# Two products of one transform unit in a single VectorE instruction, in a newly ordered plan

## The chip, the cores and the metric

The kernel runs on one core of one Trainium2 chip. The metric is the device time of one launch in microseconds. The kernel before the change took 190.81 us, the median of three runs (190.63 to 191.04).

## The reference

Two branches read the same normalised input and are multiplied at the end.

```python
xn = layernorm(A_q)                                  # [1, 2048, 640]
# branch A: a short causal convolution of k, times v, then a long convolution
k_shift = sum over t of k_pad[:, t:t+S, :] * shift_k[:, 3-t]
kv = k_shift * v
y  = irfft2(rfft2(kv padded to 2S) * rfft2(ssm_k padded to 2S))[:S]
s  = xn * (y + kv * ssm_D)
# branch B: a dense layer with gelu, a second one, then silu
h  = gelu(xn @ w1 + b1)                              # 640 -> 1728
g  = silu(h @ w2 + b2)                               # 1728 -> 640
out = A_q + s * g
```

All tensors are bfloat16; S is 2048 and D is 640.

## The kernel before, in words

The long convolution is done as a transform written as matrix products. A first stage (steps `kf` for the filter, `uf` for the signal) multiplies by sine and cosine matrices; its results go to DRAM scratch (`ks`, `us`) and come back transposed (`fl`, `ml`). A second stage works in 40 units of 128 x 512. For the filter, `ff` is a unit's transform on TensorE and `fe` its copy from PSUM to SBUF, which makes `K`. For the signal, `mu` is the transform; its result is multiplied with two things: with `K` (step `mp`, `product_a`) and with `ks`, which is `K` with neighbouring partitions exchanged (step `mq`, `product_b`). The exchange is done by two DMAs on the SyncE queue (step `mk`, `swap_load`). The two products then go through the inverse transform, `ma` on the first and `mb` on the second, which add up in one PSUM bank; `me` copies that out, `ms` stores it to scratch on GpSimd's queue, `yl` loads it back on SyncE's queue, and `y` is the last transform. `yt` multiplies it with the input, `yo` adds, `ys` and `gs` store.

Unit `i` covers 512 columns of a pair of half-slots. When `i % 5 == 2` it straddles two slots, and its operand has two pieces of 256. When `i % 3 == 2` ScalarE first copies `mu`'s PSUM bank to SBUF (`mv`, `u_copy`), and both products read that bfloat16 copy; for the other 27 units both products read PSUM in float32.

The second-stage matrices are block-diagonal, four blocks of 32 x 32. So each of `ff`, `mu`, `ma` and `mb` is four small matmuls (`blocks`, line 451), called a quad here. The string `TURNS` gives each unit a digit that says which of the four column groups each row group writes; quads with different digits use different tiles of the array. The dense branch fills the rest of TensorE: `h` is one column block of the first layer (line 504, or 500 for the last block of a chunk), `he` its gelu on ScalarE, `g` a row block of the second layer (line 537), `ge` its silu on ScalarE, `gm` the product on VectorE or GpSimd. The input comes in four chunks: `ls`, `lv`, `lr`, `lb`, `ln` normalise one, `tt` and `te` transpose it. `cv` are the 32 large VectorE steps of the short convolution. `kt` and `kc` transpose the filter.

The order of all work is written out by hand in the string `PLAN`: about 1,100 steps, each a kind, a number and, after a dot, the engine or form (`.a` ScalarE, `.d` VectorE, `.p` GpSimd for copies and products; `.f` and `.q` for quads, which act alike unless the digit is 0 and the form `f`). Each engine and each queue issues its instructions in the order in which the plan names them; semaphores hold them until their inputs are there. Eight PSUM banks (`ones`) and 48 SBUF slots (`Slots`) are handed out while the plan is read, first freed first granted, so the order of the plan also decides who waits for whose buffer.

```python
def copied(i):
    return i % 3 == 2
def one(key):
    return banks[:, ones.take(key, 2 if key[0] == "mu" and not copied(key[1]) else 1), :]
```

Of the kernel before, what the change touches and what calls it, by code (L numbers as in the profile page):

```python
# [38 lines left out]
ke13.a kc12.d gm1.d kf37 kc3.a kf5 kt13 X3 kt15 kc7.d kf3 kf30 ke37.a kf4 kc2.d kf23 ke12.a K1 kc13.d kf31 ke3.a ke4.a
d kt11 kt6 gm0.d kc15.d kt8 ke31.a ke30.d kc11.a kt9 kc6.d kc8.d kc9.a ke5.d kt14 kc14.d kt5 kf34 V1 ke23.a kf35 kf18  # L40
K2 V6 kf26 kc5.d kt0 ke34.a kf14 ke26.a kc0.d ke14.a kf33 kf38 kf45 ke45.a kf43 ke43.a g3 V4 kf15 ke35.a kf36 cv6 ks1
ke33.a kf2 V2 kf22 ke18.a ge3 kf1 ke38.a ke2.a ks11 kf0 ke1.a cv16 kf21 ke0.a g5 ke15.d ke22.a V0 kf44 ke36.a ir ke21.a
cv17 kf46 ge5 gm3.d kf10 ke10.a kf32 kf16 kf17 ke44.a ks12 cv18 ke16.a ks0 kf19 ke32.a cv7 ke19.a ke46.a g7 kf9 kf7
# [10 lines left out]
ue47.a ue42.d ue41.a fl4 us15 ue39.a us14 ue40.a ls11 ue21.d uf37 ls8 ue37.a g13 ff8.f fl7 gm6.d ff0.f lv2 ge13 fe0.a
ff6.q ff19.f ff24.q ff5.q fe5.d us12 ff9.q ls13 g9 fe9.a us7 lr2 fe24.a fl5 ff14.q fe19.a ff11.f ge9 lb2 ff18.q ln11.d
fl14 fl12 fe14.d gm8.d ff28.f fe18.a fe28.d fe8.a fe6.a us13 ln10.d mk3 g15 fe11.a ff13.q ln9.a fl6 fe13.a ff29.q ml3
ff35.f ml2 ff10.q ff34.q ff26.q fe26.a mk2 gm13.p fe35.a ln8.d g10 tt12 ge15 fe34.d fe10.d tt11 tt14 tt13 fe29.a ls15
ff2.f ff36.q ge10 te14.a ff32.q ff23.f ml4 te12.d te11.d te13.d ff30.f ls14 ff33.f fe2.a gm15.p ff12.q fe23.d fe32.a
fe30.a fe12.a mk5 ff3.f g11 ff15.q ff16.q ls12 ff17.q fe3.a fe36.d fe33.a ge11 tt10 fe15.d fe16.a ff1.q fe17.a lv3 lr3
mu8.q ff4.q te10.d mu9.f gm11.p fe4.a ff20.q mu7.f mu5.f mq9 fe1.d mv8 mq7 h30 ml5 mv5 h31 h34 mk4 mp9 mu6.q fl15 lb3  # L60
ff25.f ml0 mp5 mp8 mu11.q he30 fe20.d mk1 mu12.q he31 ma9.f ff22.q mp7 mq5 mb9.f mq6 he34 h38 mu10.f fe25.a mv11 me9.a
mp6 ff21.q mk0 fe22.a ma7.f ff37.q fe21.a gm10.p ln12.d mp12 mp10 mb7.f he38 mq10 mu14.q ln13.d mv14 mp11 me7.a fe37.a
h35 h33 ma5.q mu1.q mq12 ln14.d mb5.f ml6 mu0.f he35 ma10.f mu13.q mq1 he33 ff38.q fe38.a me5.a ma6.f mb6.f ml1 mp14
mp1 ml8 mp0 mb10.q h41 me10.a ml12 he41 me6.a h28 mq0 h36 mu3.f he28 ff39.q ml13 mu20.q mu2.q he36 mu4.f mp13 h32 mq13
mk6 ff31.f mk8 mv20 mq3 mk13 mp3 ma3.f mq14 mv2 ma0.f mu15.f fe39.a ml9 mu32.f mb3.f mb0.f ml10 mk9 he32 me0.a mq4
fe31.a mk12 me3.a h29 mp2 h37 mk7 mq15 h39 mv32 ma2.q mq11 he29 mu33.f ma14.q q6 ma12.f mp4 he37 he39 mq2 mb14.q mp15
mp32 mu23.f mq8 mb2.f mb12.f ml15 h40 mp20 mv23 ml14 me2.a mq33 mp33 mu30.q ln15.d me12.a mp23 me14.a mu21.q ma1.q
ma8.q ma11.q mq21 mb1.q mb8.q mb11.q tt16 te16.d mk10 he40 me1.a g17 tt15 mp21 mq20 mu31.q me8.a mp30 mu22.q mq30
# [21 lines left out]
def kernel(  # L90
# [85 lines left out]
    REACH = 24  # L176

    class Slots:
# [40 lines left out]
    def flat(key, uses=1):  # L219
        return rows_of[:, slots.take(key, uses), :]  # L220
# [35 lines left out]
    def full(ap, i):  # L256
        return ap if i % PER != PER // 2 else ap.rearrange("p (a b) -> p a b", a=2)
# [456 lines left out]
    def product(i, x):  # L714
        name = ("K", "ks")[x]
        u = p_part(i, 1) if copied(i) else full(one(("mu", i)), i)
        nc.vector.tensor_tensor(out=p_part(i, x), in0=u, in1=span(name, i), op=ALU.mult)  # L717
# [239 lines left out]
```

## Time and profile before

| what | value |
|---|---|
| median of three runs | 190.81 us |
| profiled execution | 190.82 us |
| its span, first to last instruction | 189.0 us |
| granted TensorE clock | 0.996 |
| TensorE busy | 182.8 us, 97% |
| VectorE busy | 166.6 us, 88% |
| ScalarE busy | 158.5 us, 84% |
| GpSimd busy | 62.3 us, 33% |

The profiled execution took 190.82 us, of which 189.0 us are the span; so 1.8 us lie outside it. Busy time of VectorE and ScalarE counts from an instruction's start to the end of its last write; the next instruction can start before that. So the distance from one start to the next, called the pitch below, is shorter than the duration, and it is the pitch that says how much work an engine gets through.

### The profile page before, as it was taken

How to read it: one execution, taken by the hardware profiler on the slowest of the kernel's cores; microseconds unless marked ns; L12 is line 12 of the kernel's file. 1: busy time of each engine (PE TensorE's matmuls, PEld its weight loads, DVE VectorE, ACT ScalarE, POOL GpSimd, SP SyncE). 2: the span in 40 equal slices, each digit the busy share in tenths (PEclk: the TensorE clock that was granted, in tenths of full speed). 3: DMA queues.
4: the chain of work that ended last, by engine and by line, in shares of the span. 5: the costliest groups of instructions: out<-in, count | busy, mean ns of one | idle time of the engine just before them, and what ended most of it. 6: DMA issues, size and time to landing. Idle time of an engine off the chain costs nothing.

```text
span 189.0 us, 4812 instructions
## 1 busy us (share of the span) xinstructions
PE 182.8 (97%) x1808; PEld 110.2 (58%) x1808; DVE 166.6 (88%) x317; ACT 158.5 (84%) x309; POOL 62.3 (33%) x98
## 2 busy tenths in 40 slices
PE   6899999999999999999999999999999999999992
PEld 2486468977764455665653344465645544677671
DVE  7979899999999999999999999999999600489993
ACT  3757999899999999999999999999898989952021
POOL 8545200029845104157216000030596620010320
PEclk9999999999999999999999999999999999999998
DMA  5999999959899899989789999699799869992545
GB/s 188 376 370 314 347 398 410 358 166 395 329 361 364 287 321 381 297 337 350 236 263 278 341 316 328 229 360 332 234 342 326 317 201 300 394 399 94 212 160 188
DMA packets 26399, 57.67 MB, mean 305 GB/s; under 512 B 3016, under 2 KB 14857, under 8 KB 26376
## 3 DMA queue, kind: packets, MB, share of 16 engines
q1 hardware_dynamic: 21872, 39.65, 61.1%
q0 software_dynamic: 4320, 17.70, 25.4%
q8 instruction: 14, 0.23, 0.5%
q14 instruction: 9, 0.07, 0.1%
q10 hardware_dynamic: 184, 0.01, 0.1%
HBM read 33.76 MB, written 18.35 MB: 276 GB/s over the span
## 4 chain that ended last, share of the span: by engine, by line
PE 85%; DVE 5%; DMA 4%; ACT 3%; issue 1%; SPq 0%; DVEq 0%
PE banks L537 31%; PE banks L504 24%; PE banks L588 9%; PE banks L451 7%; DMA w_sb<-in_B_w_dram 4%; PE banks L832 4%; PE banks L577 3%; PE banks L759 2%; PE banks L760 2%; DVE area L146 2%; PE banks L488 1%; ACT area L145 1%; DVE area L717 1%; PE banks L500 1%; DVE st L458 1%
## 5 line engine op out<-in xcount | busy, mean ns | idle before, releaser
L145 ACT CAST area<-banks 128x512 bf16<-128x512 f32 (+2 forms) x153 | 74.5, 592 | 2.8 <-PE banks L451 1.8
L537 PE MATMUL banks<-w_sb,hT 128*128 128x320 bf16 (+1 forms) x462 | 65.7, 295 | 0.0
L537 PEld LDWEIGHTS <-hT 128*128 128x128 bf16 x462 | 43.7, 98 | 18.1 <-issue 1.9
L504 PE MATMUL banks<-xnT,w_sb 128*128 128x512 bf16 x230 | 53.3, 379 | 0.1
L504 PEld LDWEIGHTS <-w_sb 128*128 128x128 bf16 x230 | 21.7, 98 | 26.7 <-issue 3.5
L516 ACT ACTIVATE hT<-banks,b_f 128x512 bf16<-128x512 f32 x52 | 32.7, 707 | 2.8 <-PE banks L832 1.7
L717 DVE TENSOR_TENSOR area<-banks,area 128x512 bf16<-128x512 f32 x54 | 34.6, 686 | 0.1
L545 ACT ACTIVATE sl<-banks 128x320 bf16<-128x320 f32 (+1 forms) x33 | 14.6, 451 | 14.8 <-PE banks L537 12.9
L553 POOL TENSOR_TENSOR xn<-xn,sl 128x320 bf16<-128x320 bf16 x13 | 10.6, 827 | 48.9 <-ACT sl L545 26.0
L641 DVE TENSOR_TENSOR area<-area 128x2560 bf16<-128x2560 bf16 x16 | 23.5, 1485 | 0.6 <-DMA area<-in_A_k_dram 0.5
L768 DVE TENSOR_TENSOR area<-banks,xn 128x426 bf16<-128x426 f32 (+1 forms) x18 | 10.0, 596 | 14.0 <-PE banks L760 14.0
L451 PE MATMUL banks<-area,mats 32*32 32x512 bf16 x640 | 18.8, 380 | 0.6 <-DVE area L146 0.5
L637 DVE TENSOR_TENSOR area<-area 128x2560 bf16<-128x2560 bf16 x12 | 17.9, 1492 | 0.2
L603 POOL DMA_DIRECT2D scrK<-area x16 | 8.9, 560 | 24.3 <-DVE area L146 18.4
L588 PE MATMUL banks<-area,WB 128*128 128x426 bf16 (+1 forms) x64 | 15.5, 299 | 0.0
L614 POOL DMA_DIRECT2D scrU<-area x16 | 8.7, 547 | 20.6 <-ACT area L145 20.6
L588 PE MATMUL banks<-area,WA 128*128 128x428 bf16 (+1 forms) x64 | 15.4, 298 | 0.0
L146 DVE CAST area<-banks 128x512 bf16<-128x512 f32 (+2 forms) x23 | 14.2, 638 | 0.3 <-ACT area L145 0.2
L451 PEld LDWEIGHTS <-mats 32*32 32x32 bf16 x640 | 6.7, 88 | 10.7 <-issue 8.9
L744 POOL DMA_DIRECT2D scrC<-area x16 | 11.7, 734 | 3.0 <-ACT WB L674 1.4
L717 DVE TENSOR_TENSOR area<-area 128x512 bf16<-128x512 bf16 x26 | 10.5, 420 | 0.0
L458 DVE BATCH_NORM_STATS2 st<-xn 128x6 f32<-128x320 bf16 x24 | 10.4, 476 | 0.0
(109 smaller groups left out, 218.6 us busy)
## 6 DMA issues: line engine op xcount, KB each, us to landing
scrK<-area POOLq DMA_DIRECT2D x16, 320.0 KB, 4.1
scrU<-area POOLq DMA_DIRECT2D x16, 320.0 KB, 3.6
area<-scrK SPq DMA_DIRECT2D x16, 320.0 KB, 6.2
area<-area SPq DMA_DIRECT2D x32, 160.0 KB, 4.2
area<-scrU SPq DMA_DIRECT2D x16, 320.0 KB, 5.6
scrC<-area POOLq DMA_DIRECT2D x16, 320.0 KB, 4.5
area<-scrC SPq DMA_DIRECT2D x16, 320.0 KB, 7.0
area<-in_A_ssm_k_dram SPq DMA_DIRECT2D x5, 512.0 KB, 9.0
```

Source lines behind the costliest of these rows:

```text
L145: return nc.scalar.copy(out=out_ap, in_=in_ap)
L146: return nc.vector.tensor_copy(out=out_ap, in_=in_ap)
L451: nc.tensor.matmul(out=out[b, :], lhsT=mats[a, m, a], rhs=rhs[a, :], start=start, stop=stop)
L458: nc.vector.bn_stats(out=st[:, j, h, :], in_=xn_tiles[c][:, j, h * HALF:(h + 1) * HALF])
L504: nc.tensor.matmul(out=ps, lhsT=w1_sb[:, t, ft * P:(ft + 1) * P], rhs=xnT[:, t, :], start=(t == 0), stop=(t == DT - 1))
L516: nc.scalar.activation(out=hT[:, ft, :], in_=one(("h", i)), func=ACT.Gelu_apprx_tanh, bias=b1_f[:, ft:ft + 1], scale=1.0)
L537: nc.tensor.matmul(out=ps[:, 0:ws.stop - ws.start], lhsT=hT[0:M, ft, q * P:(q + 1) * P], rhs=w2_sb[0:M, ft, hs.start + ws.start:hs.start + ...
L545: nc.scalar.activation(out=sl[:, ws], in_=one(key)[:, 0:ws.stop - ws.start], func=ACT.Silu)
L588: nc.tensor.matmul(out=ps[:, dst], lhsT=(WA, WB)[r][:, n2, :], rhs=rows[:, n2 % 2, src], start=True, stop=True)
L637: nc.vector.tensor_tensor(out=uc, in0=uc, in1=tmp, op=ALU.add)
L641: nc.vector.tensor_tensor(out=tmp if s else uc, in0=kh[:, r0:r0 + KR, :].rearrange("p (a b) d -> p a b d", a=2), in1=w_exp[:, j:j + 1, Non ...
L717: nc.vector.tensor_tensor(out=p_part(i, x), in0=u, in1=span(name, i), op=ALU.mult)
```

## The change

For the 32 units with `i % 5 != 2` (`joined`), the steps `mp` and `mq` become one step `mm` (`product_ab`): one VectorE instruction of 128 x 2 x 512, whose first input is the transformed signal repeated twice, and whose second input is a two-piece view of `K` and `ks`. The view needs the two slots within 2^15 elements of each other, so `Slots.beside` picks slots for `ks` near those of `K`; where it finds none, two instructions are used as before. Which of the two lies lower in memory decides the order of the halves (`swapped`). The eight straddling units keep `mp` and `mq`. The plan is a different order of all steps, with other engines for some copies, and `TURNS` is new.

```diff
-TURNS = "303222211332100321313102031211323202233020231231"
+TURNS = "123121012012312302321300020110231032133023221311"
 PLAN = ...   # another order; 1099 steps become 1067
...
+    NEAR = 25
...
+            if key[0] == "ks":
+                got = self.beside(key[1])
+                keys = [(key[0], key[1] & ~1), (key[0], key[1] | 1)]
+            elif key[0] in SPANNED:
...
+        def beside(self, g2):
+            ke, ko = self.at["K", g2 & ~1], self.at["K", g2 | 1]
+            for j in range(1, len(self.free)):
+                for i in range(j):
+                    lo, hi = sorted((self.free[i], self.free[j]))
+                    if hi - lo <= REACH and abs(lo - ke) <= NEAR and abs(hi - ko) <= NEAR:
+                        return [lo, hi]
+            first = self.free[0]
+            return [first, next(s for s in self.free[1:] if abs(s - first) <= REACH)]
...
+    def joined(i):
+        return i % PER != PER // 2
...
+    def product_ab(i):
+        k, ks = span("K", i), span("ks", i)
+        swap = int(ks.offset < k.offset)
+        lo, hi = (ks, k) if swap else (k, ks)
+        if hi.offset - lo.offset >= 1 << 15:
+            product_a(i)
+            return product_b(i)
+        both = bass.AP(lo.tensor, lo.offset, [list(lo.ap[0]), [hi.offset - lo.offset, 2], [1, HB]])
+        u = p_part(i, 1) if copied(i) else one(("mu", i))
+        out = flat(("p", i))[:, 0:2 * HB].rearrange("p (x c) -> p x c", x=2)
+        nc.vector.tensor_tensor(out=out, in0=u[:, None, :].to_broadcast([P, 2, HB]), in1=both, op=ALU.mult)
+        swapped[i] = swap
+        drop_span("K", i)
+        drop_span("ks", i)
```

Of the steps that have a choice of engine, the new plan puts these counts on each:

| step | before | after |
|---|---|---|
| `fe` on ScalarE / VectorE | 29 / 11 | 32 / 8 |
| `me` on ScalarE / VectorE | 39 / 1 | 35 / 5 |
| `ke` on ScalarE / VectorE | 45 / 3 | 44 / 4 |
| `ue` on ScalarE / VectorE | 40 / 8 | 39 / 9 |
| `kc` on ScalarE / VectorE | 4 / 12 | 5 / 11 |
| `ln` on ScalarE / VectorE | 1 / 11 | 0 / 12 |
| `gm` on VectorE / GpSimd | 19 / 13 | 17 / 15 |

More of the change, by code (lines that the diff above doesn't have):

```diff
@@ L39 @@
[L39 to L43, printed above, removed]
@@ L54 @@
[L54 to L58, printed above, removed]
@@ L59 @@
[L59 to L68, printed above, removed]
@@ new lines @@
+kc11.d kt1 kf22 kt15 K1 te5.d kc1.d ke22.a V6 kf21 ke21.d kt2 kc2.d d kt4 kf23 kc8.a kc15.a kf35 ke35.d ke23.a kf33 kt5
+kc4.d kt3 kc3.d ke33.a kf45 kt6 kf34 kc6.d ke45.a kt12 kc12.d kf46 ke34.a kf10 ke46.a kf26 kf8 ke8.a kt9 kc5.d kt10 ks7
+gm0.d kf42 ke26.d kf5 kc9.a X2 kc10.d ke5.a kt0 ks11 kf44 ke44.a kc0.a kf6 cv8 kf9 ke42.a kf7 g7 kf30 cv6 kf47 ke6.a
+ke7.a kf17 kf3 kf4 ks2 ke9.a cv17 ke30.a g1 ge7 kf12 kf13 ke17.a kf31 ke4.a ke3.a ks1 ke47.a X3 ks14 ke10.a kf25 kf32
+kf15 ge1 ke13.a ke31.a V5 kf24 ke24.a g6 kf16 kf19 ke15.a gm7.d V3 kf36 ke32.a cv7 uf5 ke25.a kf38 ke12.a kf20 ke16.a
@@ new lines @@
+ke36.a ue5.a kf14 ke20.a cv16 cv18 cv19 ke14.a kf1 ke19.a K3 ke1.a g2 ke38.a gm5.d kf18 kf29 uf2 kf40 ks15 kf37 ks8
+ke18.a cv9 kf11 g4 ke37.a V7 kf0 ks5 ks4 cv20 ke11.a ue2.a ge2 kf28 gm1.d cv21 cv22 kf27 kf2 ge6 ke29.a V2 ke40.a ke0.a
+ks6 ke27.a ks3 ke2.d uf3 ks12 kf39 h18 kf41 ue3.a ke39.a uf1 cv10 ks10 ke41.a ge4 V4 uf0 cv23 ks0 uf4 ke28.a ue1.a h23
+uf11 ue4.a uf10 ue10.a ue0.d h15 h26 he18 uf7 ue7.a he26 uf9 h24 ks13 he23 ks9 uf33 uf35 ue11.a h22 fl0 fl12 uf30 cv11
+h20 ue35.a he22 he15 ue33.a fl7 uf32 he24 gm6.d uf34 he20 fl3 h19 h21 ue34.a ue32.a cv12 ue30.a he19 uf24 fl1 fl4
@@ new lines @@
+ue24.a he21 fl2 h25 uf27 uf28 ue27.a uf6 ue6.a ue9.a uf31 cv24 us1 cv13 gm2.d he25 ue28.a h14 cv14 he14 cv15 uf19 h16
+uf25 ue19.a fl9 cv25 us0 he16 uf14 h17 us11 uf13 ue14.a uf26 he17 fl8 cv26 cv27 uf8 h27 ue8.a us2 ff7.f ue25.d ue26.d
+fl13 ue31.d ue13.a ff11.f uf29 uf21 uf12 fe7.a ue12.a cv28 he27 g14 uf20 ue21.d cv29 fl15 ge14 uf16 ue20.d uf18 cv30 g9
+ue29.a uf17 us3 ue16.a uf23 us10 uf15 fe11.a us4 uf22 g13 ue18.a cv31 ge9 uf36 ls12 ue15.a ue17.a us8 gm14.p ue22.a
+uf45 ue23.a uf43 ge13 ue45.a ue36.d uf37 us9 uf47 us5 us6 ue43.d uf42 uf38 gm13.p ue37.a ue42.a uf40 us7 ue40.a uf41
@@ new lines @@
+uf46 ue38.a uf44 ue46.a ls8 uf39 g15 ls9 fl10 fl6 ue39.d ue47.a ue44.a ff8.q ff2.q ff5.f ls10 ue41.a gm4.d us15 ge15
+us14 ff9.q fe9.a ff0.f ff34.q fe34.a fe2.a ff22.q ls11 g11 gm15.p us13 fe22.a ff24.q ff10.f fe5.d ge11 ff30.f fl5 us12
+fe8.a ls14 mk3 ff31.q g8 ff18.q fe10.a lv2 fe0.a ls13 ff13.q fe24.a lr2 fe31.a fl11 fl14 ff6.q fe18.a ff25.f g10 fe6.a
+ff4.q ml3 ge8 ff3.f gm11.p ff33.q ff12.f ls15 fe25.d ff1.f lv3 fe30.a gm9.d lb2 fe13.a ln11.d ml2 mk2 ff20.f ge10 fe4.a
+ln8.d g12 ml8 fe1.a fe3.a ln10.d lr3 fe20.d fe33.d lb3 ln9.d tt14 tt12 ln15.d gm8.p ml4 ml5 fe12.a mk4 ln13.d te12.d
@@ new lines @@
+ff26.q ge12 ff14.q te14.a fe14.d ff15.f ml0 fe15.a ff28.q tt13 tt10 te10.d fe26.a mk0 tt11 te11.d ff23.q ff36.f ml1
+fe28.a ff29.q te13.d fe36.a fe23.d ff16.q ff32.f fe16.d fe32.a fe29.a h31 ff37.f ff27.f mk12 fe37.d gm10.p mu9.q mu6.q
+he31 mu7.f mp7 mu8.q mk5 mq7 h28 h39 mm9 fe27.a h29 ma7.f mu10.f mv8 he39 he28 ma9.q ff17.f fe17.a mu14.q mb9.q mb7.f
+mm8 mv14 h30 mm6 h40 mm10 mk1 mu0.f ln12.d me9.a he29 ml13 he30 me7.d ma6.q ma10.f mm0 he40 mu11.f mv11 mb6.q ln14.d
+mb10.f ff21.q ml12 mu1.f h38 me6.a me10.a mu12.q ma8.q mm1 fe21.a mk8 mu5.q ma0.f mb8.q h33 mu4.q mv5 he38 mu3.f mu20.f
@@ new lines @@
+ir me8.a mm11 ml9 he33 mq12 mb0.f me0.a ff19.f h36 mp12 fe19.a mv20 mu2.f mu13.f ff35.f fe35.a h37 mk13 ff38.q ff39.q
+mm4 mv2 mu30.q mm3 ma4.q mu32.f he36 mm14 he37 mm13 mb4.q fe38.a fe39.a mk6 h32 mp2 h35 mk9 me4.a he32 mv32 h34 mm5 mq2
+ma12.f mu33.q he35 mm30 ma5.q mu24.q he34 ml11 ma14.f mm33 mb12.q ml6 me12.a ma13.q mb13.q ma3.q me13.a mk10 ml10 mb3.q
+mb5.f me3.a mb14.f me5.a h41 mm24 ma11.q ml7 mu31.q ma2.q mb2.q me14.a mb11.f mu22.q tt15 q2 mm31 tt18 me11.a gm12.p
+mq22 ms2 te15.d he41 g17 te18.a me2.d ma1.q ma31.q mu15.f ma33.q mk11 mp22 mb33.q mm20 mm15 mu23.q ge17 mv23 mb1.f
@@ new lines @@
+me30.a mp37 ge18 ma16.q mv38 mu28.f ma17.f mb23.q q1 mm29 me23.a ma18.q mm28 mb17.f mb27.f mb16.q mb18.f h50 ma37.f
+ma29.q me27.a ma28.q me18.a ms9 me16.d mb28.f mm38 mb29.q mb37.q me17.a ms6 me28.a ma19.f mu39.q mb19.f me19.a q3
+mu36.f mm35 q7 ms7 g22 ge22 ms12 h48 gm20.p ms10 mm36 me29.a ma36.f ma35.q mm39 ma39.q ma38.f ms11 mb36.f me37.a ip1
+ia1 mb35.f ip3 mb39.q me35.d me36.a mb38.f h55 me39.a ia3 is1 ib1 ic1 ms14 me38.d is3 ib3 g23 h53 ms15 h43 ge23 h45 yl7
+yl6 yl13 ic3 he53 h51 h47 he47 h54 h46 he45 he54 ip2 he46 yl14 he51 he43 h44 he50 h49 yl5 h42 gm23.p he44 he42 he49 yl4
@@ new lines @@
+yl0 y9 h52 y11 he48 he55 y20 y10 ia2 he52 g26 y6 ip0 y7 is2 ia0 is0 y8 yt20 yt9 yl2 yt6 ib0 yt11 ic0 g27 ge26 yt7 y21
+ib2 yl3 yl12 yt8 y19 yt10 yo2.d yo3.d yt19 yt21 gm26.d gm18.p yl1 g28 ic2 ge28 y0 y2 ys3 y1 yt2 yt0 ge27 gm22.p yl9 y4
+yt1 y3 yt3 y5 g30 yo0.d yt5 y18 yl8 y13 ge30 yt4 yo1.d ys1 y14 yl11 y17 gm27.d yt17 yl15 gm28.d y23 y12 yl10 y15 q6
+yt13 yt12 y22 yt23 yt14 g29 yt22 ga31 gm30.d ga26 ys2 y16 ge29 yt15 ga27 ys0 q4 ga30 gs27 yo4.d g24 yt18 ga28 yt16
+yo5.d gs30 ge24 g25 ge25 ys4 gm29.d g31 ga29 gm25.d gm24.d ga25 gs29 ga24 gs25 ys5 ge31 gm31.d gs31
@@ L266, in one @@
     def one(key):
-        return banks[:, ones.take(key, 2 if key[0] == "mu" and not copied(key[1]) else 1), :]
+        return banks[:, ones.take(key, 2 if key[0] == "mu" and not copied(key[1]) and not joined(key[1]) else 1), :]
     def one_bf(key):
@@ L705, in u_f2 @@
         drop_span("uin", i)
+    swapped = {}
     def p_part(i, x):
+        x ^= swapped.get(i, 0)
         return full(flat(("p", i))[:, x * HB:x * HB + HB], i)
@@ L715, in product @@
         name = ("K", "ks")[x]
+        last = x == 1 or not joined(i)
         u = p_part(i, 1) if copied(i) else full(one(("mu", i)), i)
@@ L718, in product @@
         drop_span(name, i)
+        if last and not copied(i):
+            ones.drop(("mu", i))
+    def product_ab(i):
[12 more added lines that the diff above has]
+        drop_span("ks", i)
         if not copied(i):
```

41 lines of the change are left out of this document (9 added, 32 removed).

## The prediction

> **What bounds the kernel now.** I read the page first: the busy shares, the slices, the chain that ended last.
>
> ```profile
> span 189.0 us, 4812 instructions
> PE 182.8 (97%) x1808; PEld 110.2 (58%) x1808; DVE 166.6 (88%) x317; ACT 158.5 (84%) x309; POOL 62.3 (33%) x98
> ...
> PE   6899999999999999999999999999999999999992
> ...
> DVE  7979899999999999999999999999999600489993
> ACT  3757999899999999999999999999898989952021
> ...
> PE 85%; DVE 5%; DMA 4%; ACT 3%; issue 1%; SPq 0%; DVEq 0%
> ```
>
> All three engines are nearly full, VectorE (DVE) until slice 31 (about 149 us), and TensorE (PE) carries most of the chain. So the question is how much of PE's time is work and how much is waiting for the other two. The chain in order of time answers it, since it shows PE's pace for each kind of step:
>
> ```profile
> 16.62 1.08 PE banks L504 x5
> 17.70 0.67 PE banks L500 x10
> ...
> 24.95 0.67 PE banks L488 x12
> ...
> 31.79 1.56 PE banks L577 x25
> ...
> 80.63 1.90 PE banks L537 x14
> 82.53 2.36 PE banks L588 x17
> ...
> 86.80 0.58 PE banks L451 x27
> ...
> 89.44 0.36 PE banks L451 x16
> ...
> 92.47 1.29 DVE area L146 x2
> ...
> 101.47 1.28 DVE area L717 x2
> ...
> 111.25 1.08 ACT area L145 x2
> ...
> 122.81 2.02 PE banks L537 x14
> ...
> 161.42 0.09 PE banks L759
> ...
> 185.44 0.31 ACT sl L545
> ```
>
> The plan's PE work runs from 16.62 to 185.44, 168.8 us. Its work at these paces: 46 `h` of 1.08, 4 short ones of 0.67, 32 `g` of 1.90, 96 units `kf` and `uf` of 0.18 (the 17 matmuls in 2.36 us, four matmuls to three units), 24 `y` of 0.36, 80 transposes of 0.062 and 60 of 0.056: 147.8 us. Then the quads. Four quads with four different digits start together and the run ends after 0.36 us; seven quads, of which digits come twice or thrice, take 0.58. So I count a run of neighbouring quads as 0.32 us after its last start and 0.21 for each time it waits for a digit's tiles to come free, read off `TURNS` in the plan's order. Before has 22 runs, 16.3 us. Sum 164.1: PE would end at 180.75 if it never waited, and it ends at 185.44. **So 4.7 us are waiting**, and no change of VectorE alone can give back more. Where it lies: up to 91 us the chain is on PE; from 92.5 to 114.5 it runs for long stretches over DVE and ACT; step `g17` starts at 122.81, where PE's own work would have brought it at 119.2, 3.6 late. So most of the waiting lies between 92 and 123, when chunk 3 is normalised while the first products run.
>
> **What VectorE has to do.** Its pitch from the timeline, and the groups of the page:
>
> ```profile
> 13.51 1.22 DVE L344 TENSOR_SCALAR area<-area 128x2048 int32<-128x2048 int32 x1
> ...
> 111.47 4.28 DVE L717 TENSOR_TENSOR area<-banks,area 128x512 bf16<-128x512 f32 x7
> ...
> 119.39 1.09 DVE L717 TENSOR_TENSOR area<-area 128x512 bf16<-128x512 bf16 x3
> ...
> 145.41 0.42 DVE L717 TENSOR_TENSOR area<-area 128x512 bf16<-128x512 bf16 x1
> ```
> ```profile
> L717 DVE TENSOR_TENSOR area<-banks,area 128x512 bf16<-128x512 f32 x54 | 34.6, 686 | 0.1
> L641 DVE TENSOR_TENSOR area<-area 128x2560 bf16<-128x2560 bf16 x16 | 23.5, 1485 | 0.6 <-DMA area<-in_A_k_dram 0.5
> L768 DVE TENSOR_TENSOR area<-banks,xn 128x426 bf16<-128x426 f32 (+1 forms) x18 | 10.0, 596 | 14.0 <-PE banks L760 14.0
> ...
> L717 DVE TENSOR_TENSOR area<-area 128x512 bf16<-128x512 bf16 x26 | 10.5, 420 | 0.0
> ```
>
> One product from PSUM lasts 686 ns, but seven take 4.28 us: a pitch of 0.60. From SBUF: 420 ns, three in 1.09, a pitch of 0.33. Adding the pitches of all VectorE steps in the plan's order up to the last product gives 127.8 us (32 `cv` of 1.41 and 80 products of 41.0 together make two thirds). It passed from 13.51 to 145.7, 132.2 us. So VectorE came 4.4 us later than its work asks, and it was never idle long. Its work alone would bring the last product at 141.2; PE's own work needs it at 141.4. Slack of 0.2 us on paper, 4.4 us of lateness in fact: this is where PE's waiting comes from.
>
> **The change, part by part.**
>
> The joined products. From 426 to 512 elements PSUM products grow by 90 ns, 1.05 ns an element; so 1024 elements last 686 + 536 = 1.22 us, pitch 1.13, against 1.20 for two: 0.065 saved on each of 22 units, 1.4 us. From SBUF, 512 to 2560 elements cost 1065 ns more, 0.52 ns each; two products make 0.60 instead of 0.67, 10 units, 0.7 us. Sum 2.1 us, not the 32 x 0.15 that the durations suggest, since the end of one instruction already lies under the start of the next. The bounds: 0 (if the two-piece view costs as much as it saves) and 32 x 0.15 = 4.8.
>
> For this price the Trainium skill, "VectorE: DVE Perf Modes", section "The TRN2 errata", has 58 cycles fixed for an SBUF source and 120 for PSUM. By it the estimate would be 22 x 125 + 10 x 60 ns = 3.4 us, 1.3 more than by the pitch, and the sum below 188.9 instead of 189.6. For SBUF the pitch agrees (65 ns); for PSUM it shows half, and I keep the pitch.
>
> Other steps moved onto and off VectorE before its last product: `me` +3 (1.8 us by a pitch of 0.60), `fe` -3 (-1.8), `ke` and `ue` +1 each (+1.0), `ln` +1 (+0.35), `kc` -1 (-0.4), `gm` -1 (-0.2), one `ip` behind the last product (-0.6). Sum +0.1. So VectorE has 125.9 us before its last product, 1.95 less, and could bring it at 139.4.
>
> The new order for PE. 24 runs of quads instead of 22, with other digits: 16.8 us by the same count, +0.46. This is on PE's path whatever else happens. PE has 125.8 us of work ahead of the last product's matmuls, 1.0 more, so it needs them at 142.4. The slack grows from 0.2 to 3.0 us; for the products from 100 on it is 2.6 to 3.0 wherever it is smallest, against 0.2 to 1.2 before. Only where chunk 3's transposes feed `h31` it shrinks, from 3.1 to 2.1.
>
> ScalarE. Its sum to the end is 1.5 us shorter, but at the start of `g17`, where chunk 3's first layer must be done, its own work stands 2.1 us ahead of PE's need, 2.2 before: no relief where the waiting is. Its pitches:
>
> ```profile
> 143.54 2.06 ACT L145 CAST area<-banks 128x512 bf16<-128x512 f32 x4
> ...
> 156.09 6.06 ACT L516 ACTIVATE hT<-banks,b_f 128x512 bf16<-128x512 f32 x10
> ```
>
> (0.48 and 0.59 us.) GpSimd gets two `gm` more, 1.7 us on an engine a third busy.
>
> Waits that are added. A joined product waits for `ks` as well as `K`, and `ma` waits for 1.22 us instead of the first 0.69; whatever VectorE has queued behind a late `ks` waits too.
>
> ```profile
> area<-area SPq DMA_DIRECT2D x32, 160.0 KB, 4.2
> area<-scrC SPq DMA_DIRECT2D x16, 320.0 KB, 7.0
> ...
> 148.74 2.17 POOL L744 DMA_DIRECT2D scrC<-area  x3 [1.42 <-ACT WB L674]
> ...
> 153.78 8.98 SPq L751 DMA_DIRECT2D area<-scrC  x13
> ```
>
> The exchange lands in 4.2 us. Between the last `fe` of a pair and its first use of `ks` lie 5.6 us of work at least in the new plan (`mk2`, a straddling unit), 8.9 for a joined one; 7.6 at least before. Covered; price 0, and up to 2 us for one that slips. I followed the slot rule through the plan: all 32 units find slots in reach, mostly the first two on the list, so it makes no buffer wait that first-freed would not.
>
> The round trip through scratch C. After the last quad PE has 15.3 us to fill until `y7` at 161.42 (last quad at 146.1). The new plan leaves 13.9. The trip: last stores at 150.2, loads from 153.8, landing 7.0 by the median, so 14.7 with everything; but ScalarE brought that last copy late, at 148.9, and the new plan gives it to VectorE, then idle, about 1.4 us sooner. 13.3 against 13.9: covered, barely. Head and tail (16.6 us ahead of the plan; 3.6 from PE's end to the span's) keep their work.
>
> **The sum.** Waiting now 4.7. By VectorE's slack, if it comes as late as before, 4.4 less 2.6 or 2.1 leaves 1.8 to 2.3; by ScalarE, whose slack is unchanged, about 3.6 at `g17` and 4.0 in all. The chain of 92 to 114 has both, so I take the middle, 3.0: a gain of 1.7. Less 0.46 for the quads: 1.2. PE ends at 184.2, the span is 187.8, and with 1.8 outside it 189.6, 0.6% under 190.82 (the profiled execution stands within 0.01 of the median). The ends of this case: 1.2 us of waiting, 187.8; 4.0 and a little back, 190.4.
>
> **The rivals.**
>
> ScalarE sets the waiting, VectorE's time goes idle. Then 4.0 to 4.7 of waiting plus 0.46: 190.5 to 191.2, no difference. For it: ACT at 9 in every slice from 4 to 30, and its part in the chain at 111. Against: DVE has twice as many pieces there.
>
> Slower: the order's own waits. The trip through C is the place: if the last stores go out as late as before after the last quad, `y` comes 0.8 to 1.4 us late, PE has nothing left to fill with, and with no gain elsewhere the time is 191.3 to 192.6. It decides once stores and loads together take over 13.9 us. For it: a load of C takes 7.0 us, an exchange 4.2. Against: the earlier last copy.
>
> Slower: the ten units from SBUF lose their fast rate, because their first input repeats. At 1.05 ns an element a joined one has a pitch of 1.13, 5.3 us more on VectorE; the slack goes from 3.0 to -2.3, waiting to 6.7 or more, the time to 193.3. It decides when a joined SBUF product lasts over about 1.0 us. Against: L641 repeats its weight row four times and still does 0.52 ns an element. The Trainium skill, same page, section "Mode 2×_1P", asks for 16-bit data and a step of 1, and a repeated half isn't one; the row of L641 speaks for the inner step alone counting.
>
> **How the numbers follow.** Chances: the forecast 0.56; ScalarE rival 0.18; own waits 0.19; lost rate 0.07. 0.2% is 0.4 us, about what can be told here. Faster holds the forecast case and little else, 0.56; same 0.18; slower 0.26. The forecast's own range is 187.8 to 190.4; for 8 in 10 it must reach over the second case and half of the third: 187.7 to 192.0.
>
> **What would show it.** Products of 128x1024 with 1.22 us from PSUM and 0.69 from SBUF; the chain between 92 and 114 more on PE than now; `g17` less late; the last product near 143 instead of 145; quads with 24 ends; `y` following the last `h` without a gap. I'm wrong if VectorE idles in that stretch while PE still waits for ScalarE, if PE waits for a load of C near 160, or if SBUF products last 1.2 us.

## The result, and the profile after

| kernel | median of the runs | profiled execution | its span |
|---|---|---|---|
| before | 190.62 us (190.16 to 191.26) | 190.82 us | 189.0 us |
| after | 192.34 us (191.56 to 193.51) | 192.19 us | 190.4 us |

The change makes the kernel slower: after against before is 1.0087, 95% interval 1.0066 to 1.0109, 1.7 us. The forecast was 189.6. Further on, "after" also gets 192.37 and 192.04 in two more executions. Some executions below were disturbed (`b_joined` and `a_gm` have one of 473 and 373 us, which was the profiled one); these two profiles are not read, and the ratios leave disturbed runs out.

The page of after, the same lines as those shown of before: span, busy shares, slices of PE, VectorE and ScalarE, and the shares of the chain that ended last.

```profile
span 190.4 us, 4799 instructions
PE 182.4 (96%) x1808; PEld 110.7 (58%) x1808; DVE 167.3 (88%) x286; ACT 157.9 (83%) x306; POOL 62.8 (33%) x100
...
PE   7999999999998999999999999999999999999990
...
DVE  7989899999699999999999999899999900499992
ACT  3767998999997999999999999999896978961020
...
PE 53%; DVE 23%; DMA 7%; ACT 7%; issue 5%; SPq 2%; POOL 1%; DVEq 0%; POOLq 0%
```

PE carries 53% of the chain instead of 85%. The larger part of VectorE's 23% lies at the start, up to 33 us, and at the end, where the chain stays on VectorE from 165.60 until the last stores. In between, new are slice 10 of VectorE (a 6, at about 50 us) and slice 12 of PE (an 8, at about 57 us), where before has nines. The chain in order of time says what stands there and in the stages that the prediction read:

```profile
44.49 6.72 DMA scrK<-area
51.33 1.49 DVE area L656
52.82 1.40 DVE area L652
...
57.31 0.61 DVE area L144
57.95 0.52 PE banks L603 x3
...
95.78 0.19 SPq L715
96.03 1.20 SPq L715
97.34 0.52 SPq L709
97.91 5.31 DMA area<-scrU
103.22 1.27 DVE area L736 x2
104.49 1.14 DVE area L751
...
149.90 10.79 PE banks L519 x50
160.70 0.18 PE banks L795
```

The store of scratch K holds VectorE's step `cv9` until 51.33, and six steps later PE. Between 95 and 105 the chain runs through SyncE's queue and a load of scratch U into the products. The last `h` run ends at 160.69 and `y` starts at 160.70: the trip through scratch C is covered.

The products are what was forecast. In the groups by shape of VectorE (busy, mean ns | idle):

```profile
L751 DVE TENSOR_TENSOR area<-banks,area 128x1024 bf16<-128x1024 f32 x22 | 26.1, 1216 | 0.6 <-ACT hT L531 0.6
...
L751 DVE TENSOR_TENSOR area<-area 128x1024 bf16<-128x1024 bf16 x10 | 7.2, 733 | 0.0
```

All 32 joined units are there, 1.22 us from PSUM; the 733 is a mean of nine of 0.68 and one of 1.20, which comes up below. From start to start a joined product takes 1.134 us from PSUM (two single ones 2 x 0.598) and 0.600 from SBUF (2 x 0.333): 0.062 and 0.066 saved, against 0.065 forecast, 2.0 us in all. So VectorE has the time that was promised. Where it went shows in VectorE's waits up to the last product, after and then before:

```profile
DVE area L656 <- ACT area L143: 1.5, 1, 1.5
DVE nb L486 <- POOL rs L482: 0.9, 1, 0.9
DVE area L751 <- ACT hT L531: 0.6, 1, 0.6
DVE area L144 <- ACT area L143: 0.2, 1, 0.2
```
```profile
DVE xnT L146 <- PE banks L823: 0.8, 1, 0.8
DVE area L641 <- DMA area<-in_A_k_dram: 0.5, 1, 0.5
DVE area L146 <- ACT area L145: 0.5, 2, 0.2
DVE b_f L900 <- ACT xnT L145: 0.3, 1, 0.3
```

and in its timeline, beside GpSimd's, at three places of after:

```profile
79.94 1.48 DVE L652 TENSOR_TENSOR area<-area 128x2560 bf16<-128x2560 bf16 x1
81.46 1.96 DVE L645 TENSOR_TENSOR area<-area 128x2560 bf16<-128x2560 bf16 x1
80.17 1.90 POOL L568 TENSOR_TENSOR xn<-xn,sl 128x320 bf16<-128x320 bf16 x1 [1.05 <-ACT sl L560]
...
88.89 0.90 DVE L568 TENSOR_TENSOR xn<-xn,sl 128x320 bf16<-128x320 bf16 x1
88.82 0.79 POOL L568 TENSOR_TENSOR xn<-xn,sl 128x320 bf16<-128x320 bf16 x1 [0.30 <-ACT sl L560]
...
139.54 0.68 DVE L736 TENSOR_TENSOR area<-banks,area 128x512 bf16<-128x512 f32 x1
140.14 1.20 DVE L751 TENSOR_TENSOR area<-area 128x1024 bf16<-128x1024 bf16 x1
139.98 0.81 POOL L568 TENSOR_TENSOR xn<-xn,sl 128x320 bf16<-128x320 bf16 x1
```

A `gm` on VectorE (L568) lasts 0.32 us elsewhere, here 0.90; a joined product from SBUF 0.68, here 1.20; a `cv` step 1.49, here 1.96. Each time a product of GpSimd is running when VectorE's instruction starts. The `cv` at 79.94 was there first: it keeps its 1.48, and GpSimd's product takes 1.90 instead of 0.80. A joined product from PSUM that starts in the middle of one of GpSimd's keeps its 1.22:

```profile
132.51 1.22 DVE L751 TENSOR_TENSOR area<-banks,area 128x1024 bf16<-128x1024 f32 x1
132.37 0.87 POOL L568 TENSOR_TENSOR xn<-xn,sl 128x320 bf16<-128x320 bf16 x1 [5.34 <-DMA area<-area]
```

The Trainium skill, "SBUF — State Buffer", section "Who interferes with whom", says that a VectorE instruction with two SBUF inputs and a GpSimd instruction that reads SBUF exclude each other, and that one with a single SBUF input does not; the trace agrees, with these 0.47, 0.58 and 0.52 us.

VectorE's account from 13.0 us to the end of its last product, from the trace (end taken one pitch after the last start; before 145.41, after 145.34):

| | before | after |
|---|---|---|
| idle | 2.3 | 4.4 |
| held up by a product of GpSimd | 0.3 | 1.6 |
| work | 130.1 | 127.5 |
| last product done at | 145.7 | 146.5 |

2.6 us of work less (1.95 forecast), 2.1 more of waiting, 1.3 more of standing still: 0.8 later in all. PE's last matmul ends at 185.76, before 185.41: 0.35 later. The other 1.0 us of the 1.35 in the span lies behind it. The last stores, issued on GpSimd's queue (L813, before L777) and on SyncE's (L587, before L572), after first:

```profile
182.47 0.54 POOL L813 DMA_DIRECT2D out_dram<-area  x1 [4.24 <-DVE area L809]
184.59 0.54 POOL L813 DMA_DIRECT2D out_dram<-area  x1 [1.57 <-DVE xn L568]
...
181.23 5.81 SPq L587 DMA_DIRECT2D out_dram<-xn  x5
```
```profile
182.56 1.07 POOL L777 DMA_DIRECT2D out_dram<-area  x2 [2.65 <-DVE area L773]
...
180.19 6.47 SPq L572 DMA_DIRECT2D out_dram<-xn  x5
```

Each queue's engine ends the program with a DRAIN, which the trace has among the sequencer's instructions. Before, GpSimd's lasts from its last issue at 183.10 to 188.27 and SyncE is done at 188.06. After, the last `ys` is issued at 184.59, GpSimd's DRAIN ends at 189.62, SyncE is done at 188.45. So in after GpSimd alone ends the program, 1.2 us behind everything else.

### The profile page after: what moved, and what is told of

The parts are those of the page before. It is cut to its first block, busy times and chain, and to the rows that moved or that the text cites. A ratio compares the mean times of both kernels' runs of the same rounds, so it can differ in the third digit from the quotient of the medians.

```text
span 190.4 us, 4799 instructions
## 1 busy us (share of the span) xinstructions
PE 182.4 (96%) x1808; PEld 110.7 (58%) x1808; DVE 167.3 (88%) x286; ACT 157.9 (83%) x306; POOL 62.8 (33%) x100
## 4 chain that ended last, share of the span: by engine, by line
PE 53%; DVE 23%; DMA 7%; ACT 7%; issue 5%; SPq 2%; POOL 1%; DVEq 0%; POOLq 0%
PE banks L519 17%; PE banks L552 14%; PE banks L466 6%; PE banks L603 6%; ACT area L143 5%; DVE area L656 4%; DVE area L804 4%; DMA scrK<-area 4%; DMA area<-scrU 3%; DVE area L809 2%; PE banks L850 2%; SPq L715 2%; DVE st L473 2%; DVE area L652 2%; DVE xn L568 2%
## 5 line engine op out<-in xcount | busy, mean ns | idle before, releaser
L143 ACT CAST area<-banks 128x426 bf16<-128x426 f32 (+2 forms) x150 | 74.9, 610 | 2.5 <-PE banks L603 2.0
L531 ACT ACTIVATE hT<-banks,b_f 128x512 bf16<-128x512 f32 x52 | 34.7, 733 | 4.1 <-PE banks L868 2.1
L751 DVE TENSOR_TENSOR area<-banks,area 128x1024 bf16<-128x1024 f32 x22 | 26.1, 1216 | 0.6 <-ACT hT L531 0.6
L466 PE MATMUL banks<-area,mats 32*32 32x512 bf16 x640 | 18.0, 380 | 0.0
L603 PE MATMUL banks<-area,WA 128*128 128x428 bf16 (+1 forms) x64 | 16.1, 298 | 1.5 <-DVE area L144 1.5
L144 DVE CAST area<-banks 128x512 bf16<-128x512 f32 (+2 forms) x26 | 16.0, 633 | 0.5 <-ACT area L143 0.2
L568 POOL TENSOR_TENSOR xn<-xn,sl 128x320 bf16<-128x320 bf16 x15 | 13.4, 895 | 7.5 <-DMA area<-area 5.3
L804 DVE TENSOR_TENSOR xn<-banks,xn 128x426 bf16<-128x426 f32 (+1 forms) x6 | 3.5, 595 | 10.8 <-PE banks L796 10.8
L813 POOL DMA_DIRECT2D out_dram<-area x6 | 3.3, 560 | 27.4 <-DVE area L809 20.7
```

Source lines behind the costliest of these rows:

```text
L143: return nc.scalar.copy(out=out_ap, in_=in_ap)
L144: return nc.vector.tensor_copy(out=out_ap, in_=in_ap)
L466: nc.tensor.matmul(out=out[b, :], lhsT=mats[a, m, a], rhs=rhs[a, :], start=start, stop=stop)
L531: nc.scalar.activation(out=hT[:, ft, :], in_=one(("h", i)), func=ACT.Gelu_apprx_tanh, bias=b1_f[:, ft:ft + 1], scale=1.0)
L568: mul.tensor_tensor(out=xr[:, ws], in0=xr[:, ws], in1=live["sl", i][:, ws], op=ALU.mult)
L603: nc.tensor.matmul(out=ps[:, dst], lhsT=(WA, WB)[r][:, n2, :], rhs=rows[:, n2 % 2, src], start=True, stop=True)
```

## The experiments

Names beginning with `a_` start from the kernel after, with `b_` from the one before. The kernel before, run beside them on the same chip, had medians of 190.49 to 190.63. Executions of after's family scatter by about 2 us, so profiles are used for places, and medians and ratios for sums.

**Is it the joining or the order?** `a_split` keeps after's order and issues two instructions again; `b_joined` joins in before's order, at the place of the second product (unit 35 at the first).

```diff
-        if hi.offset - lo.offset >= 1 << 15:
+        if True:                                  # a_split
```


> The changed kernel, its order kept, but each of the 32 joined steps issues two instructions of 512 again. Theory 'joining pays, the order costs': VectorE gets 2.1 us more work ahead of its last product (2 x 0.60 instead of 1.13, 2 x 0.33 instead of 0.60), TensorE waits 1 to 2 us longer between 100 and 146, time 193.3 to 194.4. Rival 'joining gives nothing' (the saved time goes idle): 192.3 within 0.3.

Measured 1.0231 (1.0166 to 1.0295) against before, about 195.0 us. By the two ratios that is 2.7 us more than after, with 1.5 and 4.0 as the ends; more than the theory had (193.3 to 194.4).

> The kernel before, its order and its digits kept, with the 32 units' two products joined at the place of the second one (unit 35 at the place of the first) and the slot rule for ks. Theory 'joining pays, the order costs': VectorE has 2.1 us less, and was the engine that came late, so TensorE's 4.5 us of waiting fall by 1 to 2: time 188.8 to 189.8. Rival 'joining costs' (later first products, waits for ks): 190.6 or more. Rival 'idle': 190.4 to 190.8.

Measured 191.62 us, 1.0038 (1.0010 to 1.0066): 0.7 us more than before, against the theory.

> The kernel before with the joined products in its own order, once more, for its profile (its time was 191.6, 1.0 above the kernel before). 'Joining moves the stall': the joined step stands at the place of the second product, so VectorE waits for ks or TensorE waits for the longer instruction; then the lateness of TensorE grows between 100 and 146 more than before (4.4 us at 146). 'Slots': the slot rule for ks makes a load wait for a buffer, then SyncE's queue shows it. 'Tail': as in the changed kernel, GpSimd's last store is later.

Measured 192.01 us, span 190.2. In the new order joining is worth about 2.7 us; in the old one it costs about 0.7. Why it costs there is not settled. VectorE's longest wait in this profile is one that before does not have, for PE's `mu`.

```profile
DVE area L752 <- PE banks L467: 1.5, 3, 0.9
```

The longest of the three, 0.9 us, ends at 110.2. Ahead of it PE itself waits 0.9 us for a load of scratch K, until 106.94, and before has no such wait either. Whether the place of the joined step or the slot rule brings this about, or whether it is the scatter, one profile does not tell.

In `a_split` the 2.0 us of the pitch come back, and there is more: two of its SBUF products are held up by GpSimd,

```profile
132.75 3.49 DVE L736 TENSOR_TENSOR area<-area 128x512 bf16<-128x512 bf16 x4
...
133.19 0.78 POOL L568 TENSOR_TENSOR xn<-xn,sl 128x320 bf16<-128x320 bf16 x1 [5.10 <-ACT sl L560]
...
134.69 0.80 POOL L568 TENSOR_TENSOR xn<-xn,sl 128x320 bf16<-128x320 bf16 x1
```

four in 3.49 us where 1.4 is usual; two of them last 1.05 and 1.61 us, 1.8 too much. With the 0.5 that after loses at 140.14 taken off, 2.0 + 1.8 - 0.5 = 3.3, inside the 1.5 to 4.0 (the profiled execution, 196.31, is 4.1 above that of after).

**The early wait.** `cv9` needs one work buffer of two slots. Followed through the plan, it gets two that the steps `ks1` and `ks2` free, whose stores to scratch K are still on their way at 50 us; in before it gets two that `ks0` and `ks6` freed. It is the new order that does this, by the rule "first freed, first granted": the new slot rule is first used at `mk3`, 246 steps behind `cv9`. `a_cv9` asks for the buffer later:

```diff
-ke18.a cv9 kf11 ... ks3 ke2.d uf3
+ke18.a kf11 ... ks3 ke2.d cv9 uf3
```


> The changed kernel with step cv9 moved on VectorE from ahead of cv20 to behind ke2, 4.9 us of work later, so it no longer waits (1.5 us at 49.8) for the store of scratch K that holds its slot, and cv20 to cv22 run in that time. Theory 'early stall carried': uf0 to uf4 start 1.2 us earlier, the gain stays up to the end, 191.0 to 191.3. Rival 'absorbed by later waits': 192.0 to 192.3.

Measured 191.59 us, 1.0051 (1.0017 to 1.0086), 0.75 less than after. The stretch of 48 to 58 us, busy time of PE, its weight loads, VectorE, ScalarE and GpSimd, after and then `a_cv9`:

```profile
48.00:58.00 10.00, 8.82 (x61) 5.65 (x60) 8.43 (x10) 9.81 (x25) 3.77 (x7) 1.00 0.84 334
```
```profile
48.00:58.00 10.00, 10.00 (x67) 6.36 (x66) 9.32 (x9) 9.81 (x26) 4.83 (x9) 1.00 0.90 358
```

PE's 1.2 us of idleness are gone. By the time alone the gain is not clear of the scatter, since the two intervals overlap. The page's own releaser for that wait in after, ScalarE, had long been done; in `a_ys_act` and `a_tail`, whose beginning is the same, the trace names the store:

```profile
DVE area L656 <- DMA scrK<-area: 1.1, 1, 1.1
```
```profile
DVE area L657 <- DMA scrK<-area: 2.6, 1, 2.6
```

Does this wait change from one execution to the next?

> The changed kernel once more, one look. Theory: the early wait of VectorE for the store of scratch K (cv9, near 50 us) changes with the landing of that store, 1.0 to 2.6 us, and the time with it by half or more of the difference. Rival: the same 1.5 us each time, and other places scatter.

> A third look at the same program as a_again1, with the same theories: an early wait of 1.0 to 2.6 us that the time follows, or the same 1.5 us again with the scatter elsewhere.

Waits of 1.3 and 1.6 us, times of 192.37 and 192.04. It changes, but in these two executions the time does not follow it: other places scatter too.

**The end of the program.** First the DRAIN by itself: before's last 40 KB store moved to GpSimd's queue.

```diff
-        nc.sync.dma_start(out=out_v[:, c * CH + q, hs], in_=xn_tiles[c][:, q, hs])
+        (nc.gpsimd if i == LAST else nc.sync).dma_start(out=..., in_=...)      # b_gs31_pool
```


> The kernel before with its very last store (40 KB, gs31) issued by GpSimd instead of SyncE. Theory 'the drain takes 5.1 us from GpSimd's last DMA issue': issue at about 186.3, drain to 191.4, span and time longer by 2.9 to 3.2 us. Rival 'the drain only waits for the stores to land': a store this small lands in about 2 us, the time is longer by 0.3 to 1.0.

Measured 194.53 us, 1.0190 (1.0138 to 1.0242): 3.9 more for one store of 40 KB, where the theory had 2.9 to 3.2. Its trace has the last issue at 186.77 and the DRAIN's end at 191.88, 5.1 us, as in before (5.2) and after (5.0). The store itself has landed at 188.63, so the rival is out.

Then after's last store, `ys5`, from SyncE's queue, and the last two, `ys4` and `ys5`, from ScalarE's, with before as the control:

```diff
-        nc.gpsimd.dma_start(out=out_v[:, 2 * i:2 * i + 2, :], in_=pair(("o", i)))
+        (nc.sync if i == 5 else nc.gpsimd).dma_start(...)             # a_ys5_sp
+        (nc.scalar if i in (4, 5) else nc.gpsimd).dma_start(...)      # a_ys_act, b_ys_act
```


> The changed kernel with one edit: its last store of a pair of rows (ys5) is issued by SyncE instead of GpSimd. Theory 'tail': the end is set by GpSimd, whose final drain lasts 5.1 us from its last DMA issue (184.56 to 189.62 in the changed kernel, 183.06 to 188.27 before), while SyncE is through at 188.45. Then the drain starts from the fifth store (182.47) and ends at about 187.6, SyncE's 188.5 sets the end, the span falls by 1.1 to 1.2 us and the time to about 191.1. Rival 'middle': the loss comes from waits of TensorE ahead of the tail; then 192.3, unchanged.

Measured 192.27 us, 1.0078 (1.0050 to 1.0106): nothing won. In its profile, a late execution (193.47), SyncE issues the 320 KB at 187.39 and its own last 40 KB at 187.90, and is done at 190.8: the cost has moved to that queue.

> The changed kernel with its last two 320 KB stores (ys4, ys5) issued from ScalarE's queue, which is idle there, in place of GpSimd's. Theory (the program ends with GpSimd's final DRAIN, about 5.1 us after its last DMA issue; SyncE is done 1.2 us earlier): GpSimd's last issue is then near 178, SyncE's end sets the span, 190.4 - 1.1 = 189.3, time 191.0 to 191.4 against 192.3, about 1.1 less than the changed kernel. Rival (the last stores land late whatever queue issues them): the last queue, whichever it is, ends near 189.6 again and the time stays at 192.0 to 192.4.

Measured 191.97 us, 1.0043 (1.0009 to 1.0077): 0.4 of the 1.1 expected, with intervals that overlap. In its profile, an execution of 190.68, SyncE ends the program at 188.14, 3.1 us behind PE, where GpSimd's DRAIN ended 3.9 us behind PE in after.

> The kernel before with ys4 and ys5 issued from ScalarE's queue: the control. Theory: GpSimd's DRAIN and SyncE's end lie 0.2 us apart there (188.27 and 188.06), so 190.3 to 190.6 against 190.5. Rival (any kernel gains by it): 189.5.

Measured 191.79 us, 1.0075 (1.0050 to 1.0101), against both expectations. In before `ys4` stands behind `ge31` in the plan; on ScalarE's queue the second of the two stores is issued only at 185.38, and SyncE's last stores, which run beside it, land after 2.6 us instead of 1.6. So the control says nothing of DRAIN; it shows small stores that land 1.0 us later beside one of 320 KB.

Something like it came out of an attempt to bring `yo4` and `yo5` forward on VectorE (in these two kernels `yo4` also runs ahead of its load `q4`, so it adds rows that are not loaded yet):

> The changed kernel with the tail of its order altered: VectorE does yt16, yo4 and yo5 right after yt15, ahead of two additions (ga27, ga30) and of yt18 and ga28, so GpSimd's last store can be issued about 1.7 us earlier (182.9 instead of 184.6); all queues keep their engines. Theory 'tail': GpSimd's drain, 5.1 us from its last DMA issue, then ends at about 188.0, SyncE's 188.4 sets the end, time 191.1 to 191.4. Rival 'no tail': 192.3, since TensorE's end and SyncE's last store stand where they stood.

Measured 193.07 us, 1.0117 (1.0085 to 1.0149).

> The changed kernel with both edits (cv9 moved, tail of the order altered). If the early stall and the tail each carry over, they add up: 189.8 to 190.3, at or below the kernel before. If only one does, 191.0 to 191.4; if neither, 192.3.

Measured 191.92 us, 1.0053 (1.0018 to 1.0089). No gain from the reordered tail in either. The load `q4`, 320 KB, came beside both stores, which landed after 4.2 us (4.3 in `a_cv9_tail`) instead of 2.5, and GpSimd's DRAIN took 6.7 and 6.8 us. So the 5.1 us are no fixed length: in these two, in before and in after alike the DRAIN ends 2.2 to 2.4 us after the last of these stores has landed.

**Both together, and the quads.**

> The changed kernel with cv9 issued behind ke2.d on VectorE (a_cv9, 191.6) and ys4, ys5 from ScalarE's queue. If the early wait of TensorE and the tail are two separate costs, the gains add: 191.6 - 1.1 = 190.5 at most, 190.2 to 190.6, level with the kernel before or a little under it. Rival (the tail is the last stores' landing): 191.3 to 191.6.

Measured 191.40 us, 1.0028 (1.0001 to 1.0055): 0.9 less than after; that the parts add fully is not shown.

The prediction counted quads as PE's own work on the path. The next three change only the digits, and in the last two every quad is four matmuls (form `.q`):

```diff
-TURNS = "123121012012312302321300020110231032133023221311"
+TURNS = "110031013232023010332233111221030223001221303313"   # a_best_q, a_cv9_ys_act_turns
-TURNS = "303222211332100321313102031211323202233020231231"
+TURNS = "321100011323213231022010123012302010332333120002"   # b_turns_q
```


> The same as a_cv9_ys_act with other digits in TURNS, chosen so that neighbouring quads repeat a digit less often: by the count of the prediction (0.32 us behind a run's last start, 0.21 for a digit that must wait) the 24 runs cost 14.6 us in place of 16.8, 2.2 less on TensorE. Theory (quads are TensorE's work and lie on the path): 0.8 to 2.2 less than a_cv9_ys_act, 188.2 to 189.6, with VectorE's lateness taking back what is missing. Rival (VectorE sets the pace, TensorE only waits longer): 190.2 to 190.6, the same as a_cv9_ys_act, with as much more waiting.

Measured 200.52 us, 1.0549 (1.0510 to 1.0587). What both sides left out: with digit 0 and form `.f` the kernel issues one full matmul of 128 rows; these digits make that of 24 quads, and neither old nor new plan has one. In the trace such a matmul starts 0.32 us after the step before it, and the next one 0.32 us after it (89.96, 90.28, 90.60). So it tells nothing of the price asked for, and was repeated with four matmuls each:

> The changed order with cv9 behind ke2.d, ys4 and ys5 on ScalarE's queue (a_cv9_ys_act, 191.4) and digits in TURNS by which the 24 runs of quads cost 14.6 us in place of 16.8, every quad as four matmuls. Theory as for b_turns_q: 0.6 to 2.2 less, 189.2 to 190.8. Rival (VectorE sets the pace): 191.2 to 191.6. If it costs more than a_cv9_ys_act, the price per repeated digit is wrong.

Measured 191.40 us, 1.0045 (1.0013 to 1.0076): the same as `a_cv9_ys_act`.

> The kernel before with other digits in TURNS and every quad as four matmuls: by the prediction's count its 22 runs of quads cost 14.6 us in place of 16.3, 1.8 less on TensorE. Theory (TensorE's own work sets the end, its waiting is fixed by when VectorE and ScalarE deliver up to 123): those gains behind 123 come out in full, those ahead of it turn into waiting; 0.5 to 1.8 less than before, 188.8 to 190.1. Rival (VectorE sets the pace everywhere until the last product): 190.4 to 190.8.

Measured 191.14 us, 1.0017 (0.9992 to 1.0043): nothing won, if not a little lost. The times are those of the rival, but the traces do not show that TensorE was given less to do. The quads' busy time, before and `b_turns_q`, then `a_cv9_ys_act` and `a_best_q`:

```profile
L451 PE MATMUL banks<-area,mats 32*32 32x512 bf16 x640 | 18.8, 380 | 0.6 <-DVE area L146 0.5
L451 PE MATMUL banks<-area,mats 32*32 32x512 bf16 x640 | 19.3, 381 | 1.1 <-DMA area<-scrK 0.5 <-DVE area L146 0.5
```
```profile
L467 PE MATMUL banks<-area,mats 32*32 32x512 bf16 x640 | 17.9, 380 | 0.0
L467 PE MATMUL banks<-area,mats 32*32 32x512 bf16 x640 | 19.2, 380 | 0.1
```

The 1.8 and 2.2 us less are there by the count alone; in the traces the quads' busy time is 0.5 and 1.3 us longer. A part of that can be quads that stand apart because they wait, so take three runs in which both chains stay on PE: 12, 9 and 11 quads take 1.18, 0.78 and 0.86 us in before (from 127.63 on) and 1.17, 0.78 and 0.86 in `b_turns_q` (from 128.17 on), with other digits. So the count's price of 0.21 for a digit that must wait is not what the traces show. That the price is wrong explains the two times as well as the rival does, and these runs cannot tell whether less work on TensorE would shorten the kernel. VectorE's last product does not come sooner either, it starts at 145.94 in `b_turns_q`.

How late PE is against its own work, counted as in the prediction from 16.62 us on, at seven places of each trace:

| us | 56 | 60 | 80 | 105 | 125 | 145 | 183 |
|---|---|---|---|---|---|---|---|
| before | -0.1 | -0.1 | 0.2 | 2.7 | 3.7 | 4.3 | 4.3 |
| after | -0.3 | 1.2 | 1.2 | 2.9 | 3.8 | 4.2 | 4.2 |
| `a_cv9` | -0.5 | -0.5 | -0.1 | 1.9 | 2.2 | 3.5 | 3.6 |
| `b_turns_q` | -0.5 | -0.5 | -0.2 | 2.8 | 5.2 | 7.0 | 7.0 |

The last row takes the quads at the 1.8 us less that the trace does not show, so 1.8 of its 7.0 may be work and not lateness.

**The products on GpSimd.** Of the five that hold VectorE up in after, four are moved to where VectorE has no instruction with two SBUF inputs:

```diff
-us8 gm14.p ... us6      -g11 gm15.p us13 ... us12      -q0 gm21.p      -ge27 gm22.p
+us8 ... us6 gm14.p      +g11 us13 ... us12 gm15.p      +q0 gm21.d      +gm18.p gm22.p ... ge27
```


> The changed kernel with four products of GpSimd elsewhere: gm14 behind us6, gm15 behind us12, gm22 ahead of ys3 (right behind gm18), and gm21 on VectorE (0.24 us there). Theory (a VectorE instruction with two inputs in SBUF stands still while GpSimd runs a product, and VectorE sets the pace): the long instructions at 81, 89, 140 and 171 go back to their usual 1.49, 0.32, 0.68 and 0.32 us, VectorE has 2.2 - 0.24 = 2.0 less, 1.3 of it ahead of its last product and 0.66 in the tail; 0.8 to 1.8 less than the changed kernel's 192.3: 190.5 to 191.5. Rival (these delays lie beside other work): 192.0 to 192.5.

Measured 1.0104 (1.0047 to 1.0161) against before: inconclusive.

> The same four moves on top of cv9 behind ke2.d and of ys4 and ys5 on ScalarE's queue (a_cv9_ys_act, 191.4). Theory: 0.8 to 1.8 less than that, 189.6 to 190.6, level with the kernel before (190.5) or under it. Rival: 191.2 to 191.5.

Measured 190.78 us, 1.0001 (0.9973 to 1.0029): 0.6 less than `a_cv9_ys_act`, level with before; the two intervals overlap, so the 0.6 alone is not clear of the scatter. Against after (1.0066 to 1.0109) the gain is clear. In its groups the joined SBUF products are all at 0.68 again,

```profile
L752 DVE TENSOR_TENSOR area<-area 128x1024 bf16<-128x1024 bf16 x10 | 6.6, 680 | 0.0
```

and nothing of VectorE is held up by GpSimd ahead of the last product. But VectorE idles 5.6 us there in that profile (a late execution, 191.97) against 3.5 in `a_cv9_ys_act`: part of what it wins it waits away. No version ran faster than before beyond its interval.

## Why the prediction was wrong, step by step

- **The price of joining** was right: 0.062 and 0.066 us a unit, 2.0 in all against 2.1, and all 32 units joined. By the Trainium skill's 120 cycles for a PSUM source ("VectorE: DVE Perf Modes", "The TRN2 errata") the estimate was 125 ns for each; the trace shows 62. The SBUF products kept their fast rate with a repeated input, as L641 had suggested.
- **"Waiting now 4.7 [...] I take the middle, 3.0"** is the term that failed. By the table TensorE's waiting is 4.2 in after against 4.3 before: next to nothing of the 1.7 us was won. That is 1.2 of the 1.6 us by which PE ends later than the 184.2 of the sum; 1.0 more lies in the tail. The next three points are what the sum put at nothing.
- **"Waits that are added"** left one out, the earliest cost of the three. I followed the slot rule for the 32 units and their `ks`, and that held; what the new order leaves on the list of free buffers for other steps, here `cv9`, I did not follow. Price: 1.5 us on VectorE, 1.2 on PE, and 0.75 of the time came back when `cv9` was moved.
- **"GpSimd gets two `gm` more, 1.7 us on an engine a third busy"** failed. Their cost was looked for on GpSimd's own time; it falls on VectorE, 1.6 us ahead of the last product against 0.3 before. That this is part of the 1.7 us is supported by `a_all`, not settled: `a_gm` alone was inconclusive.
- **"Head and tail [...] keep their work"** failed for the tail. `yo5` and `ys5` come last in the new plan, and the DRAIN behind the last GpSimd store ends the span 4.6 us after PE instead of 3.6. By the profile 1.0 us; moving the stores to another queue brought back 0.4.
- **The quads, +0.46 "on PE's path whatever else happens"**, are not borne out as a term: their busy time is 18.0 us in after against 18.8 before, and digits that the count makes cheaper were not cheaper in the trace.
- **The frame of the sum**, PE's work plus a waiting to be cut by VectorE's slack, is in doubt. The slack was reckoned from a count of VectorE's work, 127.8 us, but from 13.51 to 145.74 the trace of before has 130.2 busy and 2.0 idle: of the 4.4 us of lateness about 2 are work that the count misses. In after the work fell by 2.6 us and the last product still started at the same 145.3, since new waits took it up; that PE's waiting is what the other engines leave over, and no term of its own, fits this but is not shown. And the chain between 92 and 114 is not more on PE, as I said it would be, but on loads of scratch U, SyncE's queue and VectorE. `g17` starts 3.8 us late by the table's count, not less late than before.
- **The rivals.** The time lies in the range of "the order's own waits" (191.3 to 192.6), but that is luck for this rival: the place that it named, the trip through C, is covered, and `y` follows the last `h` at once. Whether ScalarE sets a part of the waiting is open. It does not set all of it, since moving one VectorE step took PE's 1.2 us away; VectorE's waits for ScalarE are 0.8 us in after besides `cv9`, and 1.9 in the profile of `a_all`.

The 1.7 us are closed as a sum, since `a_all`, with the three repairs (`cv9` later, `ys4` and `ys5` from ScalarE's queue, four products of GpSimd elsewhere), stands at 1.0001 of before. Open are how they divide, with a scatter of 2 us, and why the joined kernel without these costs is not faster than before.

## What to carry to other kernels

A new order of the steps is a change of its own, and often a larger one than the instruction that it was made for: go through every buffer that the new allocation hands to bystanders, every pair of VectorE and GpSimd instructions that read SBUF at the same time, and the last issue on each queue. An engine "a third busy" is not free when its instructions hold up the busiest one. And look in the trace whether a cut that a count promises was made at all: quads that the count made 2 us cheaper took as long as before.

## What the runs showed of the hardware

- GpSimd's DRAIN at the end of the program ended 5.0 to 5.2 us after its last store was issued (nine traces), and 6.7 and 6.8 where that store landed later, beside other large transfers. From the landing it is 2.2 to 2.4 us, 3.3 for the store of 40 KB in `b_gs31_pool`, which cost 3.9 us.
- A VectorE instruction with two SBUF inputs stands still while GpSimd runs a product: 0.32 becomes 0.90 us, 0.68 becomes 1.20, and in `a_split` two of 0.42 take 1.05 and 1.61. With one input in PSUM it does not: 1.22 at 132.51 in after, as elsewhere.
- One full 128-row matmul in place of four small ones in different column groups, 24 times, cost 9.1 us against `a_best_q`, which has the same digits.
